# Attention weights turned by 32 x 32 squares and a copy through DRAM, with later weight conversions spaced out

## The chip, the cores and the metric

One core of a Trainium2 chip runs the whole program. The metric is the device time of one execution in microseconds. Engines are named as in the profile: PE (TensorE matmul), PEld (its weight load), DVE (VectorE), ACT (ScalarE), POOL (GpSimd), SP (SyncE, which here only issues DMAs).

## The reference, cut to what matters

Sliding-window attention over 4 batches, 8 heads, 576 positions of 64 elements, window 64, and after it two gated two-layer networks over the 2304 tokens:

```python
scores = (q @ k.T) / sqrt(64), masked to 0 <= i - j < 64
attn = softmax(scores)
x = (attn @ v) as [2304, 512]
x = (silu(x @ w_gate) * (x @ w_val)) @ w_out              # 512 -> 1536 -> 512
out = (sigmoid(x @ w_gate2) * (x @ w_val2)) @ w_out2      # 512 -> 1536 -> 512
```

The network weights arrive as 64-bit floats (read as pairs of 32-bit words); the kernel makes float32 of them itself.

## The kernel before, in words

**Tiling.** The 2304 tokens are 18 attention blocks of 128 tokens (i = 0 to 17). They feed five token tiles of 4, 3, 4, 4 and 3 blocks (512 or 384 columns). The first network runs over the five tiles in turn, then the second network does. One pass over a tile is a stage; stages 0 to 4 are the first network's. A stage walks over 12 chunks of 128 hidden units, and each chunk is three slots on PE: the gate product `g` (12 matmuls, L429), the value product `v` (12 matmuls, L429), and the out product `a` of the chunk before (12 matmuls, L441). So a stage has 36 slots, numbered through, and slot 36 opens stage 1. Each product is made of three terms of high and low parts, so weights and activations are split into two tiles by ACT (the high part, L411 and L707) and DVE (the low part, L415 and L621).

**Order of the work.** The order on every engine is written out by hand. Three tables, `before`, `during` and `after`, say which steps are emitted ahead of a slot's product, behind it, and behind the slot's activation. Every engine and every DMA queue works strictly in its own order. `g` and `v` have one PSUM bank each, so a product waits until ACT (L696) or DVE (L705) has read the one three slots earlier. The low part of a chunk's hidden tile (L621) is emitted two slots after its `v` slot, and the out product needs it at its third matmul, four slots after that `v` slot.

**Attention inside the stages.** Blocks 0 to 3 come ahead of stage 0. While tile t is in the network, the blocks of tile t+1 are planned by `plan_attention(i, base, t, col)`: loads at base-2, q and k turned at base+1, scores on PE ahead of slot base+2 (L244), mask and row minimum on DVE after base+2 and base+3 (L263), exponentials on ACT after base+3 (L279), normalization on DVE after base+4 and base+5 (L292 to L294), the weights transposed on PE ahead of slots base+7 and base+8 (L302, four 128 x 128 transposes each) and copied out by ACT (L308), and the product with v ahead of slot base+9 or base+10 (L318), whose result is split into the next tile's x (L328, L331). For i below `TURN` (8) q and k are transposed by PE too (L202) and copied by ACT. For later blocks, q and k are copied from DRAM to DRAM into an order by 32 x 32 squares (`to_squares`, L133, two DMAs per call), loaded in that order (L145) and turned by two DVE transposes (L231).

**Weights.** The first network's weights are converted during stage 0. The second network's 36 tiles are converted in stages 2 and 3, one every two slots: a 512 KB load (L359) into one of four `raw` buffers, two ACT instructions (`round_a`, L377 and L380), four DVE instructions (`round_b`, L388 to L391), and a 256 KB store (L397). A reload (`tw`, L402) of an out-weight tile runs in every chunk. All DMAs of the stages are issued by SP; POOL issues none.

## Time and profile before

| what | value |
|---|---|
| runs | 1000.22, 1001.97, 1002.98 us; median 1001.97 |
| profiled execution | 1002.0 us, span 1000.2 us, mean granted clock 0.986 |
| stage 0 on PE | about 40.7 to 165.7 us, with the first network's conversions |
| stage 1 (384 columns, blocks 7 to 10) | 165.67 to 254.97 us |
| stage 2 (512 columns, blocks 11 to 14) | 254.97 to about 367 us |
| stage 3 (512 columns, blocks 15 to 17) | about 367 to 474 us |

The profiled execution's own time is 1.8 us above its span, which is what lies around the first and the last instruction. A time of the timeline is counted from the start of the span. A window's busy time can't exceed its length; a share of DMA near 1 means that all 16 DMA engines had packets all the time.

### The profile page before, as it was taken

To read this page: it belongs to the slowest core of one execution; us is meant where nothing else is said; L and a number is where in the kernel's file an instruction comes from. 1 tells how busy PE (TensorE), PEld (TensorE's weight loads), DVE (VectorE), ACT (ScalarE), POOL (GpSimd) and SP (SyncE) were. 2 spreads that over 40 slices of the span, in tenths; PEclk is the share of its full clock that TensorE was granted. 3 is DMA by queue.
4 is the path that set the end of the run, shared out by engine and by line. 5 is a ranking of instruction groups with operands and counts; after the bars stand their busy time and mean duration, and the time that the engine had idled before them with its cause. 6 is when DMAs were issued, how large, how long until landed. Compare 5 with 4: busy or idle time off the path is not lost.

```text
span 1000.2 us, 14684 instructions
## 1 busy us (share of the span) xinstructions
PE 980.4 (98%) x5621; PEld 844.7 (84%) x5621; DVE 515.6 (52%) x1181; ACT 457.0 (46%) x981; POOL 4.1 (0%) x20
## 2 busy tenths in 40 slices
PE   8899999999999999999999999999999999999998
PEld 6678778999888888888999888899988888888997
DVE  6999994545677768666555322233322222223322
ACT  6887785555666555655444222222222222222222
POOL 1000000000000000000000000000000000000000
PEclk7999999999999999999999999999999999999999
DMA  9658797962366667464554400020020002000100
GB/s 224 193 179 221 216 240 171 223 148 80 116 212 186 209 206 232 164 205 137 200 148 126 169 0 1 1 85 1 1 74 1 1 1 74 0 1 1 42 1 32
DMA packets 164982, 113.03 MB, mean 113 GB/s; under 512 B 102704, under 2 KB 139568, under 8 KB 164912
## 3 DMA queue, kind: packets, MB, share of 16 engines
q1 hardware_dynamic: 161264, 111.18, 38.4%
q10 hardware_dynamic: 3648, 0.92, 0.4%
q8 instruction: 44, 0.72, 0.3%
q14 instruction: 26, 0.21, 0.1%
HBM read 90.05 MB, written 27.53 MB: 118 GB/s over the span
## 4 chain that ended last, share of the span: by engine, by line
PE 86%; DVE 9%; issue 2%; DMA 1%; ACT 1%; SPq 0%; DVEq 0%
PE a L441 28%; PE g L429 27%; PE v L429 27%; DVE raw L388 2%; PE att L318 1%; DVE t L390 1%; PE att L244 1%; PE att L302 1%; DVE t L391 1%; DVE t L389 1%; DVE z L263 1%; DVE h L621 1%; DVE s L705 1%; DMA raw<-in_moe_w_val_dram 1%; DVE wv L415 0%
## 5 line engine op out<-in xcount | busy, mean ns | idle before, releaser
L429 PE MATMUL g<-x,wg 128*128 128x512 f32 (+1 forms) x1440 | 317.8, 369 | 0.7 <-ACT x L328 0.7
L429 PE MATMUL v<-x,wv 128*128 128x512 f32 (+1 forms) x1440 | 317.6, 369 | 0.0
L429 PEld LDWEIGHTS g<-x,wg 128*128 128x128 f32 x1440 | 263.3, 188 | 37.5 <-ACT x L328 0.8
L429 PEld LDWEIGHTS v<-x,wv 128*128 128x128 f32 x1440 | 261.1, 188 | 33.1
L705 DVE TENSOR_TENSOR s<-s,v 128x512 f32<-128x512 f32 (+1 forms) x120 | 75.9, 632 | 318.3 <-PE v L429 305.9
L696 ACT ACTIVATE s<-g 128x512 f32<-128x512 f32 (+1 forms) x120 | 66.5, 554 | 312.9 <-PE g L429 312.7
L441 PE MATMUL a<-h,wo 128*128 128x512 f32 (+1 forms) x720 | 166.4, 380 | 6.4 <-DVE h L621 6.4
L441 PE MATMUL a<-wo,h 128*128 128x512 f32 x648 | 157.4, 390 | 0.0
L441 PEld LDWEIGHTS a<-h,wo 128*128 128x128 f32 x720 | 132.3, 192 | 27.0 <-DVE h L621 7.6
L707 ACT ACTIVATE h<-s 128x512 fp32r<-128x512 f32 (+1 forms) x120 | 70.6, 588 | 180.6 <-DVE s L705 180.6
L441 PEld LDWEIGHTS a<-wo,h 128*128 128x128 f32 x648 | 121.3, 188 | 24.2
L621 DVE TENSOR_TENSOR h<-s,h 128x512 fp32r<-128x512 f32 (+1 forms) x120 | 76.1, 634 | 3.2
L388 DVE TENSOR_SCALAR raw<-raw 128x512 uint16<-128x512 uint16 x72 | 54.0, 750 | 9.0 <-ACT raw L377 9.0
L279 ACT ACTIVATE z<-z,nm 128x128 f32<-128x128 f32 x144 | 55.8, 389 | 2.9 <-DVE nm L263 2.7
L101 DVE TENSOR_TENSOR x<-rx,x 128x512 fp32r<-128x512 f32 (+1 forms) x20 | 12.8, 639 | 84.3 <-ACT x L100 84.3
L391 DVE CUSTOM_DVE_ANT_0 t<-raw,t 128x1024 uint16<-128x1024 uint16 x72 | 49.8, 692 | 2.5
L380 ACT ACTIVATE t<-raw 128x512 f32<-128x512 f32 x72 | 47.9, 666 | 0.0
L377 ACT ACTIVATE raw<-raw 128x512 int32<-128x512 uint32 x72 | 47.9, 666 | 0.0
L415 DVE TENSOR_TENSOR wo<-stay,wo 128x512 fp32r<-128x512 f32 x60 | 41.1, 684 | 0.0
L411 ACT ACTIVATE wo<-stay 128x512 fp32r<-128x512 f32 x60 | 37.4, 624 | 0.0
L415 DVE TENSOR_TENSOR wo<-tw,wo 128x512 fp32r<-128x512 f32 x48 | 32.9, 685 | 5.7 <-ACT wo L411 5.7
L389 DVE TENSOR_SCALAR t<-t 128x512 f32<-128x512 f32 x72 | 33.3, 463 | 0.0
(84 smaller groups left out, 562.7 us busy)
## 6 DMA issues: line engine op xcount, KB each, us to landing
raw<-in_moe_w_gate_dram SPq DMA_DIRECT2D x24, 512.0 KB, 4.2
raw<-in_moe_w_val_dram SPq DMA_DIRECT2D x24, 512.0 KB, 4.4
raw<-in_moe_w_out_dram SPq DMA_DIRECT2D x24, 512.0 KB, 3.8
tw<-k0o SPq DMA_DIRECT2D x48, 256.0 KB, 4.2
v<-in_v_dram SPq DMA_DIRECT2D x29, 256.0 KB, 4.5
out_dram<-o SPq DMA_DIRECT2D x18, 256.0 KB, 2.3
k<-ks SPq DMA_DIRECT2D x10, 384.0 KB, 5.3
k0o<-t SPq DMA_DIRECT2D x12, 256.0 KB, 2.2
```

Of the source, the lines that this page charges most:

```text
L279: nc.scalar.activation(out=z[:, hp, :], in_=z[:, hp, :], func=ACTF.Exp, scale=-1.0, bias=nm[:, hp:hp + 1], accum_out=su[:, hp:hp + 1],)
L377: nc.scalar.activation(out=lower, in_=lower.bitcast(UINT32), func=ACTF.Copy, scale=2.0 ** -29)
L380: nc.scalar.activation(out=t.bitcast(FP32), in_=upper.bitcast(FP32), func=ACTF.Abs)
L388: nc.vector.tensor_scalar(second, fourth, 0x8000, 0x4000, ALU.bitwise_and, ALU.bitwise_or)
L391: nc.vector.tensor_tensor(out=t, in0=t, in1=lower, op=ALU.add)
L415: nc.vector.tensor_tensor(out=w[:, 1], in0=mids.pop(key), in1=w[:, 0].bitcast(FP32), op=ALU.subtract)
L429: nc.tensor.matmul(out=ps[:, 0:n], lhsT=w[:, a, c, :], rhs=xt[:, b, c, 0:n], start=(j == 0), stop=(j == len(mm) - 1),)
L441: nc.tensor.matmul(out=acc[e][:, 0:n] if m == 0 else acc[e], lhsT=w[:, a, cols] if m == 0 else h[:, a, cols], rhs=h[:, b, 0:n] if m == 0 e ...
L621: nc.vector.tensor_tensor(out=h[:, 1, 0:n], in0=s, in1=h[:, 0, 0:n].bitcast(FP32), op=ALU.subtract)
L696: nc.scalar.activation(out=s, in_=gps[:, 0:n], func=(ACTF.Silu, ACTF.Sigmoid)[m])
L705: nc.vector.tensor_tensor(out=s, in0=s, in1=vps[:, 0:n], op=ALU.mult)
L707: nc.scalar.activation(out=h[:, 0, 0:n], in_=s, func=ACTF.Copy)
```

## The change

Seven edits. `TURN` is 7 instead of 8, so block 7 also takes its q and k by squares. For blocks from 7 on, the softmax weights are no longer transposed by PE and copied by ACT: DVE turns them square by square into one tile (`turn_p`, twice per block, after slot base+5), POOL's queue writes that tile to DRAM (`put_p`, one DMA of 512 KB, in slot base+6) and reads it back with the squares exchanged between partition groups (`get_p`, four DMAs of 128 KB, in slot base+7); the product with v reads the result with a strided access pattern. Both new tiles come from the four `raw` buffers. That product is now ahead of slot base+12 for these blocks, and the base of blocks 8 and later is 3 smaller, so its slot stays where it was for most of them; everything ahead of it in the block moves three slots forward. The preceding half of v goes into another buffer (`pt0`) and is loaded in slot base+7. The second network's conversions start in stage 1 (slot 38) and come one every three slots, each with its own load two slots ahead.

```diff
     NTL = len(BLOCKS)
     last = min(range(NTL), key=lambda t: (BLOCKS[t], -t))
     ORDER2 = [t for t in range(NTL) if t != last] + [last]
-    TURN = BLOCKS[0] + BLOCKS[1] + 1
+    TURN = BLOCKS[0] + BLOCKS[1]
     TILES = []
     t0 = 0
     for n in BLOCKS:
@@ -150,7 +150,7 @@

     def load_before(i, pool=None):

-        pool, eng = (pool, nc.scalar) if pool else ((qt_p, "qt"), nc.sync)
+        pool, eng = (pool, nc.scalar) if pool else ((p_p, "pt0") if i >= TURN else (qt_p, "qt"), nc.sync)
         if i:
             nat[i, "v0"] = load_tokens(v, "v0", 128 * i - W, pool, 0, eng)
         else:
@@ -308,6 +308,33 @@
         nc.scalar.activation(out=t, in_=ps, func=ACTF.Copy)
         st[i, "pt", par] = t

+
+
+    def turn_p(i, par):
+        z, _ = st.pop((i, "z", par))
+        if par == 0:
+            st[i, "zt"] = raw_p.tile([128, 4, 2, HP, 32], FP32, tag="raw", name="zt")
+        nc.vector.transpose(st[i, "zt"][:, :, par].rearrange("p j a r -> p a j r"), z)
+
+    def put_p(i):
+        d = dram.tile([4, 32, 4, 2 * HP * 32], FP32, name=f"pd{i}")
+        nc.gpsimd.dma_start(
+            out=d.rearrange("i c j e -> (i c) (j e)"),
+            in_=st.pop((i, "zt")).rearrange("p j b a r -> p (j b a r)"),
+        )
+        st[i, "pd"] = d
+
+    def get_p(i):
+        d = st.pop((i, "pd"))
+        t = raw_p.tile([128, 4, 2, HP, 32], FP32, tag="raw", name="pt")
+        for j in range(4):
+            nc.gpsimd.dma_start(
+                out=t[32 * j:32 * j + 32].rearrange("c i b a r -> c i (b a r)"),
+                in_=d[:, :, j].rearrange("i c e -> c i e"),
+            )
+        for par in range(2):
+            st[i, "pt", par] = t[:, :, par].rearrange("p i a r -> p a i r")
+
     def pv(i, pick=None):
         ps = bank(pick)
         pt = [st.pop((i, "pt", par)) for par in range(2)]
@@ -318,7 +345,8 @@
                     nc.tensor.matmul(
                         out=ps[64 * par:64 * par + 64, hp, half * W:(half + 1) * W],
                         lhsT=vv[half][:, 2 * hp + par, :],
-                        rhs=pt[par][:, hp, half * W:(half + 1) * W],
+                        rhs=pt[par][:, hp, 2 * half:2 * half + 2] if i >= TURN
+                        else pt[par][:, hp, half * W:(half + 1) * W],
                         start=True,
                         stop=True,
                     )
@@ -487,11 +515,12 @@
             fn(*a)

     def plan_attention(i, base, t, col):
-        pv_at = 10 if t == 1 or (t > 2 and col == 0) else 9
+        pv_at = 12 if i >= TURN else 10 if t == 1 or (t > 2 and col == 0) else 9
+        base -= 3 * (i > TURN)
         if base >= 2:
             at(during, base - 2, load_qk, i)
         at(during, base + 1, load_v, i)
-        at(during, base + 5, load_before, i)
+        at(during, base + (7 if i >= TURN else 5), load_before, i)
         for nm in "qk":
             if i < TURN:
                 at(before, base + 1, transpose_in, i, nm)
@@ -506,8 +535,14 @@
         at(after, base + 4, normalize, i, 0)
         at(after, base + 5, normalize, i, 1, first=True)
         for par in range(2):
-            at(before, base + 7 + par, transpose_p, i, par)
-            at(before, base + 7 + par, evacuate_p, i, par)
+            if i < TURN:
+                at(before, base + 7 + par, transpose_p, i, par)
+                at(before, base + 7 + par, evacuate_p, i, par)
+            else:
+                at(after, base + 5, turn_p, i, par, first=True)
+        if i >= TURN:
+            at(during, base + 6, put_p, i)
+            at(during, base + 7, get_p, i)
         at(before, base + pv_at, pv, i)
         at(before, base + pv_at, lambda: x_hi(i, x_of(t), col))
         at(before, base + pv_at, lambda: x_lo(i, x_of(t), col))
@@ -536,11 +571,11 @@
         convs.append((3 * fc + 5, (0, "o", fc)))
     convs = [(n - 7, key) for n, key in sorted(convs)]
     later = [(1, nm, fc) for fc in range(FC) for nm in "gv"] + [(1, "o", fc) for fc in range(FC)]
-    convs += [(2 * SPT + 2 * j, key) for j, key in enumerate(later)]
+    convs += [(SPT + 2 + 3 * j, key) for j, key in enumerate(later)]
     next_raw = [0]

     def raw_ahead(upto):
-        while next_raw[0] < min(upto, len(convs)):
+        while next_raw[0] < min(upto, 3 * FC):
             load_raw(convs[next_raw[0]][1])
             next_raw[0] += 1

@@ -555,7 +590,10 @@
     for j, (s, key) in enumerate(convs[SPLIT_EARLY:], SPLIT_EARLY):
         at(during, s + 1, round_a, key)
         at(during, s + 2, round_b, key, key[0] == 1 or key[1] == "o")
-        at(during, s + 2, raw_ahead, j + 1 + 4)
+        if key[0] == 0:
+            at(during, s + 2, raw_ahead, j + 1 + 4)
+        else:
+            at(during, s - 2, load_raw, key)
         if key[0] == 0:
             plan_split(s + 2, key)
```

## Rows read from the trace of the kernel before

**Rows 1.** Page, part 1: busy time of each engine, share of the span, instructions.
```profile
PE 980.4 (98%) x5621; PEld 844.7 (84%) x5621; DVE 515.6 (52%) x1181; ACT 457.0 (46%) x981; POOL 4.1 (0%) x20
```

**Rows 2.** Windows: us, then each engine's busy us, granted clock, DMA share, GB/s.
```profile
125.00:150.00 25.00, 22.53 (x128) 17.79 (x127) 24.38 (x61) 20.24 (x45) 0.00 (x0) 0.98 0.96 240
165.67:254.97 89.30, 89.30 (x722) 85.56 (x721) 44.28 (x137) 48.41 (x122) 0.00 (x0) 1.00 0.58 139
187.80:209.90 22.10, 22.10 (x182) 21.29 (x181) 10.77 (x35) 11.83 (x30) 0.00 (x0) 1.00 0.70 150
254.97:367.00 112.03, 111.95 (x722) 91.04 (x722) 82.34 (x205) 70.75 (x158) 0.00 (x0) 1.00 0.63 193
```

**Rows 3.** Timeline of PE, stage 1: start us, us, line, operation, tiles, count [idle].
```profile
188.54 2.24 PE L429 MATMUL g<-x,wg 128*128 128x384 f32 x12
...
194.78 2.24 PE L429 MATMUL g<-x,wg 128*128 128x384 f32 x12
196.87 0.60 PE L302 MATMUL att<-ident,z 128*128 128x128 f32 x4
197.22 2.33 PE L429 MATMUL v<-x,wv 128*128 128x384 f32 x12
199.39 0.60 PE L302 MATMUL att<-ident,z 128*128 128x128 f32 x4
199.75 2.33 PE L441 MATMUL a<-h,wo 128*128 128x384 f32 x12
202.01 1.15 PE L318 MATMUL att<-pt,v 128*64 128x64 f32 x32
...
224.15 1.15 PE L318 MATMUL att<-pt,v 128*64 128x64 f32 x32
```

**Rows 4.** Timeline of PE, stage 2.
```profile
318.89 2.89 PE L429 MATMUL g<-x,wg 128*128 128x512 f32 x12
...
321.97 3.00 PE L429 MATMUL v<-x,wv 128*128 128x512 f32 x12
324.81 0.60 PE L302 MATMUL att<-ident,z 128*128 128x128 f32 x4
```

**Rows 5.** Timeline of PE, end of stage 0: the inputs of block 7.
```profile
156.92 0.66 PE L202 MATMUL att<-ident,q 128*128 128x128 f32 x4
158.41 0.65 PE L202 MATMUL att<-ident,k 128*128 128x128 f32 x4 [0.84 <-DVE x L331]
158.82 2.99 PE L429 MATMUL v<-x,wv 128*128 128x512 f32 x12
```

**Rows 6.** Timeline of DVE, stage 1, then a conversion in stage 2.
```profile
198.06 0.55 DVE L621 TENSOR_TENSOR h<-s,h 128x384 fp32r<-128x384 f32 x1
...
204.92 0.71 DVE L231 STREAM_TRANSPOSE qt<-q 128x512 f32<-128x512 f32 x1
205.54 0.94 DVE L231 STREAM_TRANSPOSE kt<-k 128x768 f32<-128x768 f32 x1
...
297.63 0.75 DVE L388 TENSOR_SCALAR raw<-raw 128x512 uint16<-128x512 uint16 x1
...
299.73 0.68 DVE L415 TENSOR_TENSOR wo<-tw,wo 128x512 fp32r<-128x512 f32 x1
```

**Rows 7.** PE after a wait in stage 0 (timeline), and that stretch's clock (windows).
```profile
107.62 4.14 PE L441 MATMUL a<-h,wo 128*128 128x512 f32 x10 [2.12 <-DVE h L621]
...
107.60:111.60 4.00, 3.98 (x10) 3.12 (x11) 3.93 (x8) 2.21 (x5) 0.00 (x0) 0.57 0.77 218
```

**Rows 8.** DMAs: landing of L359 and of L397; L133's issue, ns; medians 110 to 150 us.
```profile
DMA to landing us min/median/max: 3.4/4.2/7.2
...
DMA to landing us min/median/max: 2.0/2.2/5.6
...
L133 SPq DMA_DIRECT2D ks<-in_k_dram x48: 550/617/1545, 82.3 to 216.7; - x48
...
raw<-in_moe_w_val_dram SPq DMA_DIRECT2D x4, 512.0 KB, 5.3
```

## The prediction

> **What bounds the kernel now.** I read the page first, then windows by stage, then the timelines of PE, DVE, ACT and SP around one attention block, and last the DMA view. PE is busy 98% of the span [rows 1], so the end is set by the sum of PE's work plus its gaps. The windows say where the gaps are: late in stage 0 DVE is busy 24.4 of 25 us and PE 22.5; in stages 1 and 2 PE is full (89.30 of 89.30 and 111.95 of 112.03), while DVE is busy 50% and 74% and DMA 58% and 63% [rows 2]. So from 165.67 us on each microsecond of PE work that goes, or each microsecond that PE has to wait, moves the end by as much, if the cover of DVE and DMA holds.
>
> **What goes on PE.** In stage 1 a block's transposes take 0.35 and 0.36 us of start-to-start time (196.87 to 197.22, 199.39 to 199.75), and the products behind them are longer than the 2.09 us of the one ahead: 2.17 for `v`, 2.26 for `a` [rows 3]. Half of the last excess I leave to the entry into the product with v, which stays. That is 0.71 + 0.08 + 0.08 = 0.87 us per block. In stage 2 `g` and the transposes take 3.08 together, so `g` 2.73, and the `v` behind them 2.84 [rows 4]; with the second half alike 0.70 + 0.11 + 0.11 = 0.92. Blocks 7 to 10 lie in stage 1 and 11 to 17 in stages 2 and 3: 4 x 0.87 + 7 x 0.92 = 9.9 us. Block 7's q and k leave PE too: 156.92 to 158.82 is 1.90 us, 0.84 of it a wait [rows 5]. In its place DVE turns both, 0.62 + 0.94 us back to back [rows 6], behind the same x_lo that ended at 158.4; it ends near 160.0, and without the transposes PE reaches the scores at 159.65. So 0.3 us of wait comes back: 1.6 gained. Together 11.5 us.
>
> **What comes on DVE and ACT.** A conversion takes DVE 2.10 us from start to start (297.63 to 299.73), the two square turns of the weights 2 x 0.62 = 1.24, read from the q turn of the same 128 x 512 form [rows 6]; the new turns write in runs of 32 elements, for which no row has a price, and I take the same (twice that is 1.24 us more per block). Stage 1 gets 12 conversions and 4 pairs of turns: 44.3 + 25.2 + 5.0 = 74.5 us in about 85.7, that is 87%. This is between stage 2's 74%, where PE shows no loss, and stage 0's 98%, where it does [rows 2]. Stage 2 falls from 18 conversions to 12 and gets 5.0 us of turns: 82.3 - 12.6 + 5.0 = 75 us, covered better than now. ACT loses the two copies per block and gains 12 conversions in stage 1; it is 48.4 of 89.3 now and stays below 70%.
>
> One point of stage 1 is late all the same. The turns are queued on DVE ahead of the chunk's low part (L621). In block 8 that low part runs 198.06 to 198.61 behind the second normalization, and the out product at 199.75 needs it 0.35 later, at 200.1: 1.5 us to spare [rows 3, 6]. The turns take 1.24 of it, and PE arrives 0.8 sooner without its transposes: 0.5 us late, in blocks 8, 9 and 10, so 1.5 us. Block 7 has a 512-column out product there and is not late. In stages 2 and 3 each slot is 0.64 us longer [rows 3, 4], and the point stays covered.
>
> **The copy through DRAM.** This is the term that decides. From the end of the turns to the product with v there are 5 whole slots and the work of other blocks. Counted from the start of slot base+3, in stage 1: the turns end at 10.8 us (198.06 + 1.24, where that slot began at 188.54) [rows 3, 6]. The new block period is 22.14 (202.01 to 224.15) less 0.87, 21.3, and the product with v starts 1.1 before its end, at 20.2 [rows 3], or at 20.7 with the 0.5 us above. That leaves 9.8 us for the copy. Block 7 has no such 0.5, but 0.6 more in its 512-column out product: 10.0. In stages 2 and 3 nine slots are 5.8 us longer, the chain before the turns only 0.6 (its first product) to 2.7 (a conversion of 2.1 in it too): 12.5 to 14.6 us are left.
>
> Its cost has no row: POOL issues no DMA before. From SP's rows: a 256 KB store lands 2.2 us after issue, 512 KB loads 4.2 [rows 8]; for the other 256 KB of the store I add 1.0, a 512 KB read is 4.2, and three more issues in series at 0.62 each are 1.9: 9.3 us. The lower end takes the fastest landings (2.0 + 1.0 + 3.4 + 1.7 = 8.1). The upper end takes the slowest landings and issues (5.6 + 1.0 + 7.2 + 3 x 1.55 = 18.4). From 110 to 150 us, where DMA is nearly full, loads land in up to 5.3, 1.1 more than the median [rows 8]. Stage 1 gets as full: I add 0.85 to the store and to the read and take 11.0, nearest to the medians. So PE waits 11.0 - 9.8 = 1.2 us in three blocks of stage 1 and 1.0 in block 7: 4.6 us; none in stages 2 and 3.
>
> The Trainium skill prices this by its own rule ("DMA: Bandwidth & Descriptors", section "Anatomy of one DMA — SWDGE (gpsimd) path"): about 2.0 us fixed per DMA plus its bytes at 436 GB/s, and little for more descriptors. As an estimate from that page, the store is 3.2 us and the four reads, overlapped, 3 to 5, so the copy would fit and the sum would be 4.6 us lower. No run here shows it yet.
>
> DMA in stage 1: between 187.8 and 209.9 us it is busy 70%, 15.5 us [rows 2]. Per block come three 512 KB loads, three 256 KB stores and the copy's 1 MB; at stage 2's 193 GB/s per 0.63 share, 306 GB/s when full, that is 3.3 MB or 10.9 us: 26 us of work in 21.3, over slots 46 to 61, where the squares of the last batch are written. About 8 us would pile up. Loads have 3.5 slots (7.7 us) and need 4.2; behind them the activation has two slots. I count this as hidden apart from the 1.7 us above, with the whole 8 as a rival. The larger squares of batch 1 (slots 12 to 27) add about 1 MB to stage 0's nearly full DMAs; DVE is the bound there and finds its loads in time, so I take 0, and at most 2 us.
>
> Edits at no cost: the product with v reads two runs of 32 columns instead of 64 in a row (no row has it; each run is contiguous; at double its 1.1 us the price would be 12 us over 11 blocks); the `raw` buffers now carry five tiles per nine slots, each free at least one slot before its turn comes, SP and POOL waiting in order; conversions end in slot 145 and the first reload of them comes in slot 143 with the earliest of them.
>
> **Sum.** 1002.0 - 9.9 - 1.6 + 1.5 + 4.6 = 996.6 us. It is made on the profiled execution (1002.0), which equals the median of the runs, 1001.97; so the forecast is 996.6 us.
>
> **Rivals.**
> *The copy lands in time everywhere* (9.8 us or less): the medians' 9.3 speaks for it, the crowded stage 1 against. 996.6 - 4.6 = 992; without the late low parts 990.5.
>
> *The copy is held behind DVE's conversion burst, and PE's clock falls*: slower. Place: stage 1, slot base+6. Right behind the turns DVE does the low part and a conversion, 2.1 us without a pause. If POOL's queue can't start its store before that burst ends, the copy is 13.1 us and PE waits 3.3 per block. After a wait of 2.12 us in stage 0, ten matmuls took 4.14 us at a granted clock of 0.57, that is partly at the 1.2 GHz level [rows 7]; ten of them at the full level take 10/12 of 2.73, 2.3 us. So each such wait costs 1.8 more. A wait of 0.84 was followed by normal matmuls [rows 5]. Four blocks: 4 x (3.3 + 1.8) = 20; 992 + 20 = 1012. It decides from a copy of about 11.9 us, where the wait reaches 2.1: 4 x 3.9 = 16, 1008. For it: DVE's runs without a gap; against: the store may be handed out within the gaps.
> A rule of the Trainium skill says just that ("SBUF — State Buffer", section "Who interferes with whom"): a DMA issued from GpSimd's queue is starved while VectorE runs a copy or tensor-with-scalar instruction in a two-port mode, and should go by another queue. The conversion is made of four instructions like these; no row shows the starving, since POOL's queue moved nothing before.
>
> *DMA becomes the bound of stage 1's middle*: 8 us more than the case in time, 1000. For it the 26 us of work in 21; against, that stage 0 ran at 0.96 [rows 2] with no wait of ACT for a load.
>
> *DVE becomes the bound of stage 1*: if stage 1 behaves as stage 0, one wait of 2.1 us and its clock loss per block: 992 + 4 x 3.9 = 1007.
>
> **How the numbers follow.** No change means within 0.3%, 999.0 to 1005.0, about what a measurement of this kernel can tell. Forecast (copy late by up to 2 us in stage 1; own range 993 to 1000) 0.38; in time (989 to 993) 0.25; held behind the burst (1006 to 1015) 0.19; DMA the bound (997 to 1003) 0.13; DVE the bound (1003 to 1008) 0.05. Faster: 0.35 + 0.25 + 0.04 = 0.64; within: 0.03 + 0.09 + 0.02 + 0.02 = 0.16; slower: 0.20. The range 990 to 1006 leaves out about 0.04 below and 0.16 above.
>
> **What would show it.** Right: no L302 in blocks from 7 on, a block period near 22 us in stage 1 and 0.9 us shorter than before in stage 2; PE waits at L318 for a DMA near 1 us, in stage 1 alone. Wrong: waits of over 2 us at L318 with a granted clock below 1 behind them, or any such wait in stages 2 and 3; no wait at all at L318 (then 992); waits of ACT at L377 or L411 for DMAs (the DMA rival); PE waits at L441 for L621 of over 1 us in stage 1 (the DVE rival). The prediction is wrong where the time is above 1006, or where a gain comes from stage 0.

## The result, and the profile after

The changed kernel takes 1016.08 us (median of 4 runs, 1014.42 to 1020.03) beside 1001.5 for the kernel before in the same measurement: a ratio of 1.0144, 95% interval 1.0111 to 1.0178. It is slower, and it lies outside the predicted range. The profiled execution is the slowest of the four, with a span of 1018.2 us; before had 1000.2.

The page first. PE's work went down by 2.4 us against [rows 1], while the span went up by 18: PE waits, and part of its work runs slower.

```profile
PE 978.0 (96%) x5525; PEld 841.6 (83%) x5525; DVE 529.9 (52%) x1205; ACT 445.2 (44%) x956; POOL 45.2 (4%) x75
```

The windows by stage say where (columns as in [rows 2]: length, busy time of PE, PEld, DVE, ACT, POOL, granted clock, DMA share, GB/s). The stages are cut at the first product `g` of each.

```profile
166.94:273.49 106.55, 91.94 (x690) 87.41 (x689) 70.57 (x190) 59.29 (x146) 13.37 (x20) 0.94 0.87 236
195.00:213.00 18.00, 17.73 (x152) 16.97 (x154) 11.10 (x27) 7.22 (x12) 2.74 (x5) 0.85 1.01 260
224.00:240.00 16.00, 12.89 (x115) 11.63 (x113) 10.23 (x25) 4.70 (x9) 3.36 (x5) 0.89 1.04 289
273.49:492.10 218.61, 214.09 (x1281) 174.51 (x1281) 144.01 (x344) 113.22 (x250) 27.79 (x35) 0.99 0.63 194
196.20:200.90 4.70, 4.70 (x33) 4.58 (x31) 2.91 (x6) 1.74 (x3) 1.11 (x3) 0.57 1.08 264
```

Stage 1 was 89.30 us with PE full [rows 2]; it is 106.55 now, 17.25 longer, with PE idle for 14.6. Stages 2 and 3 together are 218.61, against 219.2 before (254.97 to 474.2): 0.6 shorter, where the prediction had 6.4. From stage 4 on nothing changed (526.1 us, 526.0 before). Stage 0 is 1.3 longer in this profile, which is not the change: the twelve profiles taken here with block 7's inputs on squares have 121.8 to 126.4 us there, median 123.3, and the five with them on PE 125.0 or 125.1.

The timeline of PE shows the idle time of stage 1: start, duration, what it computes, and in brackets the wait ahead of it with what ended it.

```profile
181.05 1.10 PE L244 MATMUL att<-kt,qt 64*64 64x128 f32 x32 [2.81 <-DVE kt L231]
...
195.27 1.98 PE L345 MATMUL att<-pt,v 128*64 128x64 f32 x32 [4.59 <-DMA pt<-pd]
197.18 3.77 PE L457 MATMUL g<-x,wg 128*128 128x384 f32 x12
...
225.03 2.03 PE L469 MATMUL a<-h,wo 128*128 128x384 f32 x10 [0.41 <-DVE h L659]
...
233.93 1.59 PE L244 MATMUL att<-kt,qt 64*64 64x128 f32 x32 [2.70 <-DVE kt L231]
235.44 3.44 PE L469 MATMUL a<-h,wo 128*128 128x384 f32 x12
...
264.53 1.51 PE L345 MATMUL att<-pt,v 128*64 128x64 f32 x32 [3.70 <-DMA pt<-pd]
265.97 3.51 PE L457 MATMUL g<-x,wg 128*128 128x384 f32 x12
```

L345 is the product with v (L318 before), L457 and L469 are `g`/`v` and `a` (L429 and L441), L659 the low part of h (L621). Two waits are for the copy (4.59 and 3.70 us), two for the turned q and k of a block (2.81 and 2.70), and 0.8 us in all for the low part of h. Behind three of the four long ones PE is slow: `g` takes 3.77 us where [rows 3] have 2.24, at a granted clock of 0.57 (the last window row above), partly at the 1.2 GHz level. With the clock at 1.00 stage 1 has 86.3 us of PE work (v4 and v6 below); here it is 91.94. So 17.25 = 14.6 of waits + 5.6 of slow clock - 3.0 of work that went.

Why block 8's q and k are late is a matter of order on DVE (first wait above). Block 8 starts 3 slots ahead, block 7 does not, so 6 slots lie between them where the others have 9, and block 8's inputs are queued behind block 7's normalization and turns:

```profile
177.08 0.69 DVE L294 TENSOR_TENSOR z<-z,su 128x512 f32<-128x512 f32 x1
177.69 1.30 DVE L317 STREAM_TRANSPOSE zt<-z 128x512 f32<-128x512 f32 x2
178.91 0.51 DVE L659 TENSOR_TENSOR h<-s,h 128x384 fp32r<-128x384 f32 x1
179.34 0.70 DVE L231 STREAM_TRANSPOSE qt<-q 128x512 f32<-128x512 f32 x1
179.97 0.93 DVE L231 STREAM_TRANSPOSE kt<-k 128x768 f32<-128x768 f32 x1
```

Block 10's q and k are late for another reason: DVE itself stood until their loads had landed.

```profile
231.68 0.71 DVE L231 STREAM_TRANSPOSE qt<-q 128x512 f32<-128x512 f32 x1 [2.99 <-DMA q<-qs]
232.80 0.98 DVE L231 STREAM_TRANSPOSE kt<-k 128x768 f32<-128x768 f32 x1 [0.41 <-DMA k<-ks]
```

These two loads landed 5.9 and 6.3 us after their issue; in stage 1 of the kernel before, such loads landed in medians of 4.0 and 4.8. SyncE was also issuing one DMA right behind another from 218.5 to 236.8 us, so a part of the lateness can be that queue's backlog. No run separates the two.

The copy of block 7 in POOL's timeline:

```profile
179.29 0.71 POOL L321 DMA_DIRECT2D pd<-zt  x1 [172.74 <-DVE zt L317]
185.89 2.64 POOL L331 DMA_DIRECT2D pt<-pd  x4 [5.90 <-DMA v<-in_v_dram]
```

The DMA issues of stage 1 (count, KB each, median us from issue to landing):

```profile
raw<-in_moe_w_val_dram SPq DMA_DIRECT2D x6, 512.0 KB, 6.1
raw<-in_moe_w_gate_dram SPq DMA_DIRECT2D x6, 512.0 KB, 4.3
pd<-zt POOLq DMA_DIRECT2D x4, 512.0 KB, 4.7
...
pt<-pd POOLq DMA_DIRECT2D x16, 128.0 KB, 5.2
k<-ks SPq DMA_DIRECT2D x5, 384.0 KB, 6.3
```

The turns end at 179.0 and the store is issued 0.3 us later. The loads are issued at 185.89, 0.6 us after the store has landed (the view puts the wait down to another DMA of that moment), and take 2.64 us to issue. Where PE waited for the copy, the turns were 16.3 us (block 7) and 13.7 us (block 10) behind it. Raw loads of `w_val` land in 6.1 us, where [rows 8] had 5.3 in the crowded stretch of stage 0; those of `w_gate` land in 4.3.

### The profile page after: what moved, and what is told of

Its sections match the earlier page's. It is cut to its first block, busy times and chain, and to the rows that moved or that the text cites. A ratio compares the mean times of both kernels' runs of the same rounds, so it can differ in the third digit from the quotient of the medians.

```text
span 1018.2 us, 14634 instructions
## 1 busy us (share of the span) xinstructions
PE 978.0 (96%) x5525; PEld 841.6 (83%) x5525; DVE 529.9 (52%) x1205; ACT 445.2 (44%) x956; POOL 45.2 (4%) x75
## 4 chain that ended last, share of the span: by engine, by line
PE 77%; DVE 10%; DMA 5%; ACT 3%; issue 3%; SPq 1%; POOL 1%; DVEq 0%; ACTq 0%
PE g L457 25%; PE a L469 24%; PE v L457 23%; DMA pt<-pd 2%; DVE raw L416 2%; PE att L345 1%; ACT z L279 1%; DVE t L418 1%; DMA raw<-in_moe_w_out_dram 1%; PE att L244 1%; DVE t L419 1%; DVE t L417 1%; DVE z L263 1%; DVE h L659 1%; DVE s L743 1%
## 5 line engine op out<-in xcount | busy, mean ns | idle before, releaser
L457 PE MATMUL g<-x,wg 128*128 128x512 f32 (+1 forms) x1440 | 324.9, 375 | 0.7 <-ACT x L356 0.7
L457 PE MATMUL v<-x,wv 128*128 128x512 f32 (+1 forms) x1440 | 316.2, 368 | 0.0
L457 PEld LDWEIGHTS g<-x,wg 128*128 128x128 f32 x1440 | 268.7, 192 | 38.8 <-ACT x L356 0.8
L457 PEld LDWEIGHTS v<-x,wv 128*128 128x128 f32 x1440 | 262.0, 188 | 33.5
L469 PE MATMUL a<-h,wo 128*128 128x512 f32 (+1 forms) x720 | 165.6, 378 | 7.1 <-DVE h L659 7.1
L745 ACT ACTIVATE h<-s 128x512 fp32r<-128x512 f32 (+1 forms) x120 | 70.6, 588 | 199.0 <-DVE s L743 199.0
L469 PE MATMUL a<-wo,h 128*128 128x512 f32 x648 | 157.4, 390 | 0.0
L469 PEld LDWEIGHTS a<-h,wo 128*128 128x128 f32 x720 | 132.7, 192 | 28.8 <-DVE h L659 9.5
L469 PEld LDWEIGHTS a<-wo,h 128*128 128x128 f32 x648 | 121.3, 188 | 24.2
L659 DVE TENSOR_TENSOR h<-s,h 128x512 fp32r<-128x512 f32 (+1 forms) x120 | 75.9, 632 | 3.9
L359 DVE TENSOR_TENSOR x<-att,x 128x512 fp32r<-128x512 f32 x14 | 9.7, 691 | 45.4 <-ACT x L356 45.4
```

The lines of the kernel that those rows point to most:

```text
L457: nc.tensor.matmul(out=ps[:, 0:n], lhsT=w[:, a, c, :], rhs=xt[:, b, c, 0:n], start=(j == 0), stop=(j == len(mm) - 1),)
L469: nc.tensor.matmul(out=acc[e][:, 0:n] if m == 0 else acc[e], lhsT=w[:, a, cols] if m == 0 else h[:, a, cols], rhs=h[:, b, 0:n] if m == 0 e ...
L659: nc.vector.tensor_tensor(out=h[:, 1, 0:n], in0=s, in1=h[:, 0, 0:n].bitcast(FP32), op=ALU.subtract)
L745: nc.scalar.activation(out=h[:, 0, 0:n], in_=s, func=ACTF.Copy)
```

## The experiments

Theory: in stage 1 the DMA engines have more work than PE, through the conversions and the copy together, and the wait falls on whatever transfer is late. Rivals: the copy's queue on GpSimd, the order of SyncE's queue, the pressed block starts. One table for all, from window rows like those above. DMA work is the share times the length, that is the time that the packets took, per DMA engine. A packet's whole time is counted where it starts, so a share can pass 1. The work is 3.7 to 4.2 us per MB in every row, and highest in the kernel before: the crowding has not swollen it.

| kernel | stage 1 us | PE busy | DMA work us | MB | stages 2+3 us | stage 4 us | ratio to before |
|---|---|---|---|---|---|---|---|
| before | 89.3 | 89.3 | 51.8 | 12.4 | 219.2 | 75.6 | 1 |
| changed | 106.6 | 91.9 | 92.7 | 25.1 | 218.6 | 75.6 | 1.0144 |
| e1 copy, no conversions in stage 1 | 94.7 | 86.7 | 70.1 | 18.1 | 236.7 | 75.6 | 1.0215 |
| e4 conversions, no copy | 92.0 | 90.6 | 77.3 | 20.5 | 219.1 | 75.6 | 1.0025 |
| e2 product with v later | 101.0 | 91.4 | 94.9 | 25.8 | 216.8 | 75.6 | 1.0061 |
| e3 q, k earlier | 108.3 | 93.2 | 99.7 | 26.0 | 217.7 | 75.6 | 1.0143 |
| e5 copy by ScalarE's queue | 110.5 | 91.3 | 90.6 | 24.5 | 213.5 | 75.6 | 1.0128 |
| e7 a quarter of raw bytes | 99.2 | 88.3 | 78.4 | 20.7 | 212.3 | 75.6 | 1.0028 |
| e8 stores by GpSimd's queue | 110.9 | 93.3 | 98.7 | 26.7 | 225.1 | 75.6 | 1.0249 |
| e9 starts mended | 103.2 | 92.0 | 95.0 | 25.3 | 217.9 | 75.6 | 1.0095 |
| v6 | 88.7 | 86.2 | 70.1 | 18.4 | 215.6 | 76.5 | 0.9942 |

**Each half alone.** e1 keeps the copy and puts the conversions back to where they were:

```diff
-    convs += [(SPT + 2 + 3 * j, key) for j, key in enumerate(later)]
+    convs += [(2 * SPT + 2 * j, key) for j, key in enumerate(later)]
```

> The changed kernel, with the later conversions back where they were (from slot 72, one every two slots). Theory A (the copy through DRAM is slow by itself: 13 to 16 us in every block against 9.8 us available in stage 1): PE still waits 3 to 5 us at the product with v in stage 1, with the clock falling behind it; the time stays at 1008 to 1016. Theory B (early conversions tie SP's queue to the pace of VectorE and fill the DMA engines in stage 1, and both late loads and slow copies follow from that): in stage 1 the waits for q and k go and the copy fits or is late by under 1 us; in stages 2 and 3, with 4.5 loads per block instead of 3, the copy may be later than now. 990 to 1000.

1023.93 us (1021.69 to 1028.4), ratio 1.0215, 1.0172 to 1.0257: above both ranges. Stage 1 loses 5.4 us against before in place of 17.25. But in stages 2 and 3 conversions in every second slot meet the copy, and the same thing happens there. Windows of e1: stage 1, then the stretch ahead of a wait of 4.14 us, the one behind it, and the stretch ahead of a wait of 4.38.

```profile
164.76:259.48 94.72, 86.69 (x689) 82.37 (x688) 48.41 (x146) 46.62 (x124) 11.14 (x20) 1.00 0.74 191
...
290.00:309.00 19.00, 14.51 (x94) 11.10 (x94) 13.77 (x31) 6.24 (x11) 3.50 (x5) 0.94 1.05 291
309.00:325.00 16.00, 16.00 (x89) 13.32 (x86) 9.99 (x27) 10.68 (x27) 0.70 (x1) 0.85 0.24 81
...
358.00:378.00 20.00, 15.19 (x99) 11.70 (x99) 14.43 (x34) 7.07 (x12) 3.49 (x5) 1.00 1.01 286
```

The share over the whole of stages 2 and 3 is 0.68, and yet it is full ahead of each wait and nearly empty behind one: the mean of a stage hides it. In e1's stage 1, without conversions beside them, the copies of blocks 7 to 10 took 11.5, 12.7, 10.7 and 10.7 us from the turns to the last landing, and PE waited for three of them: 2.28, 1.09 and 0.97 us.

e4 is the other half, the kernel before with the later conversions in stage 1:

```diff
-    convs += [(2 * SPT + 2 * j, key) for j, key in enumerate(later)]
+    convs += [(SPT + 2 + 3 * j, key) for j, key in enumerate(later)]
```

> The kernel before, with only the later conversions moved (from slot 38, one every three slots, each with its own load). Theory A: these alone cost little, 1000 to 1004, and stage 1 keeps its 89 us. Theory B: SP's queue is tied to VectorE already, q and k come late in stage 1 and PE waits there: stage 1 is 3 to 8 us longer, 1004 to 1010.

1004.71 us, ratio 1.0025 (1.0001 to 1.0049); stage 1 is 2.7 longer, a little under theory B's 3 to 8. So the halves cost 2.7 and 5.4 us in stage 1 and both together 17.25: 9 us belong to their meeting. In DMA work: the conversions add 25.5 us, the copy 18.3, either fits into 86 to 89 us of PE work, both do not.

**Moving the wait.** e2 gives the copy two slots more, e3 loads q and k earlier:

```diff
-        pv_at = 12 if i >= TURN else 10 if t == 1 or (t > 2 and col == 0) else 9
+        pv_at = 14 if i >= TURN else 10 if t == 1 or (t > 2 and col == 0) else 9
```
```diff
-            at(during, base - 2, load_qk, i)
+            at(during, base - (6 if i > TURN else 2), load_qk, i)
```

> The changed kernel, with the product with v two slots later (14 instead of 12 slots behind the base) for blocks 7 and later, which gives the copy 4.2 us more in stage 1 and 5.4 us more in stages 2 and 3. Theory A (the copy's length is the loss): the waits at the product with v (12.7 us in the profile of the changed kernel, and some 7 us of slow matmuls behind them) go except for 1 us at most; 996 to 1002, less what the late q and k still cost. Theory B (crowded DMA and SP's queue): the waits move to other places (q and k, the raw loads), at least half of the loss stays: 1006 to 1016.

> The changed kernel, with q and k of blocks 8 and later loaded four slots earlier. If the two waits of 2.7 to 2.8 us at the scores (with 1.6 us of slow matmuls) come from SP's queue standing behind the stores of the conversions, they go, and nothing else changes: 1008 to 1012 against 1016. If they come from full DMA engines, the loads land later too, or other transfers do, and the time stays within 3 us of 1016.

e2: 1009.69 us, ratio 1.0061 (1.004 to 1.0081). No wait for the copy is left, but stage 1 is still 101.0, with waits of 2.81, 2.28 and 2.22 us for turned q and k. Of the loss in time some two fifths stay, more than theory A and less than theory B said. e3: 1018.78, ratio 1.0143 (1.0085 to 1.0202), within 3 us of 1016 as the second side had it: block 10's wait for k is gone, and the product with v waits 5.01, 3.61 and 2.95 us in stage 1. In e3 what one transfer gains another loses; block 8's 2.81 stays in both.

**Which queue.** e5 issues store and loads from ScalarE, the loads a slot later:

```diff
-            at(during, base + 7, get_p, i)
+            at(during, base + 8, get_p, i)
...
-        nc.gpsimd.dma_start(
+        nc.scalar.dma_start(
```

> The changed kernel with the copy of the softmax weights (one store, four loads for each block) issued by ScalarE's queue in place of GpSimd's; the loads are issued one slot later, so that ScalarE doesn't stand behind the store. Theory (crowded DMA engines): the copy is as long as before, 12 us or more in stage 1 from the turn to the last landing (changed kernel: 13.4 to 16.3), pv still waits there for the copy, stage 1 stays at 103 us or more (106.6) and the time at 1011 to 1020 us. Rival (GpSimd's queue and its 2.2 to 2.9 us of issuing make the copy long): the copy takes 10 us or less from turn to landing, pv's waits for it go (10.6 us in the changed kernel), stage 1 comes to 98 us or less and the time to 1007 us or less.

1016.64 us, ratio 1.0128 (1.0089 to 1.0167), no gain. Waits of PE in the changed kernel (total us, times, longest):

```profile
PE att L345 <- DMA pt<-pd: 10.6, 3, 4.6
...
PE att L244 <- DVE kt L231: 5.5, 2, 2.8
```

And the first of e5's:

```profile
PE att L244 <- DVE kt L231: 12.3, 3, 8.7
```

Neither side is right in full. PE's waits for the copy fell in stage 1 from 8.3 to 3.1 us (0.96 in block 7 and 2.12 in block 10; the view puts these down to others, but they end 0.2 and 0.3 us behind the copy's last landing), and the time did not fall. q and k of a block now come 8.7 us late: SyncE's queue, which loads them, stood for 4.4 us behind the copy's store ahead of these loads. Such waits of SyncE's queue in stage 1 of e5 (in the changed kernel there is one, of 1.3 us):

```profile
SPq L145 <- DMA pd<-zt: 6.9, 1, 6.9
...
SPq L133 <- DMA pd<-zt: 4.4, 1, 4.4
```

So e5 shows that the move to ScalarE gains nothing as it stands, not that the queue costs nothing. The store lands in 3.0 us (median) from ScalarE's queue and 3.7 from GpSimd's, the loads in 5.2 and 5.4.

e6 leaves out DRAM and moves the weights from tile to tile, in 16 pieces of 32 KB:

```diff
         for j in range(4):
...
+            for i4 in range(4):
+                nc.scalar.dma_start(
+                    out=to[32 * j:32 * j + 32, i4], in_=z[32 * i4:32 * i4 + 32, j]
+                )
```

> The changed kernel with the softmax weights moved straight from the tile of turned squares to the tile that pv reads, 16 pieces of 32 KB issued by ScalarE's queue in slot 6, in place of the store to DRAM and the four loads: half of the copy's bytes, one transfer's landing in place of two. Everything else, the later conversions in stage 1 too, as in the changed kernel. Theory (the round trip's two landings on crowded DMA engines are the loss): the move lands 6 to 9 us after the turn, pv's waits for it (10.6 us and the clock behind them) go, the waits of scores for kt (5.5 us) stay, stage 1 is 93 to 98 us in place of 106.6 and the time 1003 to 1008 us. Rival (pieces of 32 rows by 1 KB are what is slow, or 16 issues hold ScalarE): the move takes 11 us or more, or ScalarE's issues take over 3 us for each block and show as waits of scores and products for ScalarE, and the time is 1012 us or more.

1123.11 us, ratio 1.1209: the rival. ScalarE's issuing is the price, and so the move's own length was not measured under comparable conditions. Timeline of ACT's queue in e6: eleven of a block's pieces take 8.09 us to issue, 0.74 each, and PE waits 101.8 us in all for `s` behind them.

```profile
177.61 8.09 ACTq L325 DMA_DIRECT2D pt<-zt  x11
```

e8 issues the stores of converted weights from GpSimd, so that no store on SyncE waits for DVE:

```diff
-            nc.sync.dma_start(out=d, in_=tf)
+            (nc.gpsimd if key[0] == 1 else nc.sync).dma_start(out=d, in_=tf)
```

> The changed kernel with the stores of the later converted weights issued by GpSimd's queue in place of SyncE's, so that SyncE's queue has no store left that waits for VectorE's conversion in stages 1 to 3; same bytes, same copy. Rival (the order of SyncE's queue holds the loads back): loads of q and k run ahead, the waits of scores for kt behind block 8 go, stage 1 is 100 us or less and the time 1010 us or less. Theory (DMA work of 92.7 us in a stage whose PE work is 86 to 87): the loss only changes its place, to the copy's loads behind a store in GpSimd's queue or to q and k; stage 1 at 104 us or more and the time 1013 to 1020 us.

1025.91 us, ratio 1.0249, worse than either side said. Waits for k behind block 8 are gone, as the rival wanted, and the copy's loads, queued behind the stores, cost more than before (waits of PE, e8):

```profile
PE att L345 <- DMA pt<-pd: 19.8, 9, 5.0
```

SyncE's raw loads stood 18.9 us behind the copy in stage 1 (1.3 in the changed kernel); both take the four `raw` buffers. So e8 mends one queue and burdens two.

**Fewer bytes, same order.** e7 loads a quarter of each later weight and lets GpSimd set the rest to zero, so it leaves out most of the second network's weights:

```diff
-        nc.sync.dma_start(out=dst, in_=rows(key))
+        src = rows(key)
+        if key[0] == 1:
+            n, size = (256, 1024) if key[1] == "o" else (1, CC)
+            nc.gpsimd.memset(dst[:, n:size], 0)
+            dst, src = dst[:, 0:n], src[:, 0:n]
+        nc.sync.dma_start(out=dst, in_=src)
```

> The changed kernel with a quarter of each later weight's bytes loaded (128 KB of 512 KB; GpSimd sets the other three quarters to zero, so that most of the second set of weights is left out); the conversions, their stores, the copy and the whole order as in the changed kernel. The share of the DMA engines in stage 1 times its length gives 51.8 us of DMA work before, 77.3 with the conversions alone, 70.1 with the copy alone and 92.7 in the changed kernel, whose PE work in stage 1 is 86 to 87 us. Theory (stage 1 became as long as its DMA work): about a dozen conversions fall there, some 8.1 MB with their stores, of which the loads left out are 4.6 MB or so, 14 us of the 25.5; the work is then some 78 us, below PE's: stage 1 is 95 to 99 us (what the copy alone gave, 94.7, and a little), the time 1005 to 1010 us. Rival (the order of SyncE's queue: stores that stand behind VectorE's conversions hold the loads of q, k and v back, whatever the bytes): stage 1 at 103 us or more, time 1013 us or more.

1004.81 us, ratio 1.0028 (1.0008 to 1.0048). DMA work came to 78.4 us, where 78 was expected, and stage 1 to 99.2, just over the upper end (99). Stages 2 and 3 show what the change is worth with no wait in them, 212.3 us with PE busy for all of it. Windows of e7, stage 1, and stages 2 and 3:

```profile
162.27:261.51 99.24, 88.35 (x689) 84.00 (x688) 76.40 (x190) 59.18 (x146) 21.75 (x31) 0.98 0.79 209
261.51:473.83 212.32, 212.32 (x1282) 173.31 (x1281) 154.98 (x344) 113.63 (x250) 38.92 (x59) 1.00 0.52 155
```

The rival does not fit: SyncE's queue stood longer behind the conversions than in the changed kernel, and stage 1 became shorter. Its waits for them in stage 1, changed kernel first, then e7:

```profile
SPq L425 <- DVE t L419: 21.2, 6, 9.9
...
SPq L430 <- DVE t L424: 28.4, 8, 6.0
```

One thing in e7 works against it. While GpSimd sets zeros, a conversion's first instruction on DVE takes up to 2.41 us (at most 0.77 in the changed kernel), and DVE is busy for 76.4 us in place of 70.6; so the bytes alone may be worth more. Of the 10.9 us of waits left, 2.8 are block 8's, and some 4 are for copies of 11.7 to 12.2 us, from the turns to the last landing, that had room for 10.0 to 11.7.

The window of stage 1 of e9, which comes next:

```profile
162.36:265.57 103.21, 91.97 (x689) 86.91 (x688) 71.31 (x192) 62.05 (x154) 11.97 (x20) 0.95 0.92 245
```

**The starts, with the conversions left in stage 1.** e9 mends the order of the blocks:

```diff
-        base -= 3 * (i > TURN)
+        base -= {TURN: 0, TURN + 1: 1, TURN + 2: 2}.get(i, 1 if nb == 3 else 3) if i >= TURN else 0
```
with the product with v at 14 slots (13 for a stage's last block and for blocks 12 slots apart) and q and k 5 slots ahead.

> The changed kernel with the starts alone altered, as in v4: blocks 8, 9 and 10 ahead by 1, 2 and 3 slots in place of 3 each, pv 14 slots behind a block's start (13 for the last block of a stage and where blocks are 12 slots apart), q and k of blocks from 8 on loaded 5 slots ahead. The later conversions stay one in 3 slots from stage 1 on. Theory (stage 1 has 92.7 us of DMA work, so that no order of the blocks can bring it below that): the 2.8 us wait of block 8 goes, others stay or move, stage 1 is 95 to 102 us, time 1004 to 1011 us. Rival (the pressed starts were the loss, DMA work only its shape): stage 1 at 91 us or less, time 1000 us or less.

1012.08 us, ratio 1.0095 (1.0068 to 1.0121). Block 8's wait falls from 2.81 to 0.64 us, and stage 1 is still 103.2: a little above the theory's end and 12 above the rival's. The three edits together are worth 3.3 us of stage 1 here, less than e2's later product alone (5.5), so the order's own worth is not known from e9. Of its 11.2 us of waits 5.0 are for the copy, and 2.83 for a low part of h that stood on DVE behind the turns. The bytes left out in e7 are worth 7.3, and order and conversions together (v4, v6) 17.7 and 17.8.

**Versions.** v1 has stage 1 as before and the copy from block 11 on, with the conversions one in 3 slots until stage 4; v2 the copy from block 7 on, mended starts and the same conversions:

```diff
+    convs += [(2 * SPT + 3 * j, key) for j, key in enumerate(later)]
```

> Stage 1 as in the kernel before (weights of blocks 7 to 10 transposed on TensorE, no later conversion there); the turned copy through GpSimd's queue from block 11 on alone, with pv 14 slots behind a block's start (13 where blocks are 12 slots apart); the later conversions one in 3 slots from stage 2 to stage 4, in place of one in 2 slots in stages 2 and 3. Theory (the copy is long only while it shares the DMA engines with the conversions and the loads of stage 1): stage 1 is 89 to 90 us as before (89.3), stages 2 and 3 are 212 to 215 us (219.2: 7 blocks by 0.92 us less), stage 4 grows by 1 us at most, time 993.5 to 998 us. Rival (the copy, DVE's turns and the new waits eat up what TensorE is spared, wherever they stand): stages 2 and 3 at 218 us or more, or stage 4 longer by 3 us or more, time 1000 us or more.

> The changed kernel with three things altered: the later conversions one in 3 slots from stage 2 to stage 4 (none in stage 1), pv 14 slots behind a block's start (13 where blocks are 12 slots apart), and the starts of blocks 8, 9 and 10 moved ahead by 1, 2 and 3 slots in place of 3 each, so that block 8 isn't pressed against block 7. Theory (what is lost in stage 1 is the DMA's crowding by conversions beside the copy, and the pressing of block 8 by a fixed 2.8 us): stage 1 is 85 to 89 us (106.6 in the changed kernel, 89.3 before), stages 2 and 3 are 212 to 215 us, time 989 to 996 us. Rival (stage 1 is full even without conversions, so that q, k and the copy hold one another up): stage 1 at 93 us or more with waits of 2 us and longer left on kt or on the copy, time 998 us or more.

v1: 1000.88 us, ratio 0.9989 (0.9968 to 1.001). Stage 1 is 89.4 as expected, stages 2 and 3 216.1 and stage 4 78.0, both over what I expected: PE waited 1.62 and 2.04 us for low parts of h that stood on DVE behind a conversion and a stage's output tiles, and 1.74 ahead of block 14's product with v, for which the trace names no cause. v2: 1011.1, ratio 1.0079 (1.0053 to 1.0104): the rival's figures, stage 1 95.6, because block 8's k, loaded 2 slots ahead, landed late (4.46 us); stages 2 and 3, at 220.5, are 5 over too, with three waits of 1.5 us for a low part of h among others.

v3 and v4 are these with the conversions one slot earlier, the output weights in every second slot of stage 4, and in v4 q and k 5 slots ahead:

> As v1 (stage 1 as before, the copy from block 11 on alone, pv 13 or 14 slots behind a block's start) with the later conversions moved by one slot against the h's low part (one in 3 slots through stages 2 and 3 for gate and value weights), and the output weights one in 2 slots from the 8th slot of stage 4. Theory (what v1 lost against 212.7 us of PE work in stages 2 and 3, and the 2.4 us of stage 4, were low parts of h that stood behind a conversion or behind stage 4's first output tiles): stages 2 and 3 213 to 215 us, stage 4 75.6 to 76.6, time 995 to 998 us, 0.4 to 0.7% below the kernel before. Rival (VectorE's turns hold the low part of h back by themselves): waits of 1.5 us for each block stay, stages 2 and 3 at 216 us or more, time 999 us or more.

> As v2 (the copy from block 7 on, no conversion in stage 1, blocks 8, 9 and 10 ahead by 1, 2 and 3 slots) with the conversions where v3 has them, q and k of blocks from 8 on loaded 5 slots ahead of a block's start in place of 2, and pv 13 slots behind the start for the last block of a stage. Theory (without conversions stage 1 has 70 us of DMA work beside 86 of PE; v2's 4.5 us wait was block 8's k, loaded too late): stage 1 86 to 89 us, stages 2 and 3 213 to 216 us, time 991 to 996 us. Rival (in stage 1 transfers come in bunches, so that any earlier load makes another one late): stage 1 at 92 us or more, time 998 us or more.

Both missed, in the main for one reason: v3 1003.94 us (1.0024, 1.0007 to 1.0041), v4 1005.33 (1.0047, 1.0025 to 1.0068). Stage 4 grew to 80.7 and 81.8, with waits of 0.3 to 1.1 us for a low part of h. Stage 1 did what was expected, 89.3 in v3 and 88.8 in v4; stages 2 and 3 were 0.2 and 2.3 over, at 215.2 and 218.3. So v5 and v6 start the conversions 10 slots ahead of stage 2 and leave nine, one in 3 slots, for stage 4:

```diff
+        (2 * SPT - 10 + 3 * j if j < 27 else (NTL - 1) * SPT + 6 + 3 * (j - 27), key)
```

> As v3, with the later conversions one in 3 slots from 10 slots ahead of stage 2 on (27 of them up to the end of stage 3), and the last 9 one in 3 slots from the 6th slot of stage 4. Theory (v3 lost 5 us in stage 4 to low parts of h behind a conversion in every second slot): stage 1 89.3 to 90.5 us, stages 2 and 3 214 to 216 us, stage 4 75.6 to 77 us, time 994.5 to 998.5 us beside 1000 to 1002 of the kernel before. Rival (conversions cost in stage 4 what they spare before it, at any spacing): stage 4 at 78 us or more, time 999 us or more.

> As v4 (the copy from block 7 on), with v5's places for the later conversions and q and k loaded 5 slots ahead for blocks 8 to 10 alone. Theory: stage 1 88.5 to 90.5 us (3 conversions at its end beside the copy), stages 2 and 3 214 to 216.5 us, stage 4 75.6 to 77 us, time 993.5 to 998 us. Rival (the three conversions beside block 10's copy bring the waits of stage 1 back): stage 1 at 92 us or more, time 999 us or more.

v5: 999.53 us, ratio 0.997 (0.995 to 0.999); its stages are as expected (89.6, 215.0, 75.6), the time is 1 us above. v6: 996.76 us (993.28 to 1000.76), ratio 0.9942 (0.9925 to 0.9959), in every range of its theory and faster than both kernels. Windows of v6, stage 1, and stages 2 and 3:

```profile
167.09:255.81 88.72, 86.23 (x689) 82.29 (x688) 51.20 (x151) 51.71 (x136) 11.11 (x20) 1.00 0.79 207
255.81:471.45 215.64, 212.93 (x1282) 173.52 (x1281) 146.60 (x351) 110.73 (x241) 25.13 (x35) 1.00 0.66 197
```

The copy is in all of v6's blocks from 7 on, by GpSimd's queue as in the changed kernel. The clock stays at 1.00, and 2.5 and 2.7 us of waits are left.

## Why the prediction was wrong

**The step that failed** is the DMA sum of stage 1. The prediction worked out 26 us of work in a period of 21.3 and 8 us of pile-up, and then went on: "I count this as hidden apart from the 1.7 us above". It was not hidden: stage 1 has 92.7 us of DMA work beside 86.3 of PE work. In the prediction's terms for stage 1: PE waits 8.3 us for the copy, where 4.6 were in the sum; 5.5 for the turned q and k, where there was nothing (2.8 of them, block 8's, are not DMA's, see below); 0.8 for the low part of h, where there were 1.5. That makes the 14.6 us of waits. The 5.6 us of slow clock behind them were in a rival only. The rival that took the 8 us whole had the place right and the price too low by more than half; and its sign, waits of ACT for raw weights, shows once, with 2.1 us. What came late were the copy and block 10's q and k. Stage 0, on which I leaned (share 0.96, no wait of ACT for a load), issues its raw loads four conversions ahead; the copy had no such lead.

**The copy at 11.0 us**: from the turns to the last landing it was 16.1, 11.8, 11.8 and 13.5 us in stage 1, against 11.5, 12.7, 10.7 and 10.7 in e1 and 9.8 to 14.1 in v4, both without conversions there. So 11.0 was near for e1, where PE waited 4.4 us in all for it (4.6 in the sum), and not for the changed kernel. The addition for a crowded stage, 1.7 us on top of 9.3, is the mis-sized term: it was 2.5 to 6.8. The room was predicted at 9.8 to 10.0; it was 10.0 in block 10, and 11.7 in block 7. Stages 2 and 3 were to have no wait for it: copies of 11.3 to 15.0 us met a room of 12.7 to 14.4, block 11 waited 2.29 and block 16 2.10 us.

**Block 8** was not seen. The prediction gave blocks 8 to 10 one period; the first of them has 6 slots and not 9. That is 2.81 us in the changed kernel and in each of e1, e2, e3, e5, e6, e7 and e8, which leave the starts alone, with conversions beside them or not.

**PE's transposes.** Predicted 0.92 us per block in stages 2 and 3, 6.4 in all: PE busy 219.15 before, 212.3 to 212.9 in e7, v1 and v6, so 6.2 to 6.8. Right. Stage 1: 3.5 predicted, 3.0 measured (89.3 to 86.3). The product with v reads its runs of 32 at no cost, as counted (median 0.222 us for one of its matmuls, before and after). The changed kernel got 5.1 of the 6.4 in stages 2 and 3 as PE work and lost 4.5 in waits.

**Block 7's inputs**, 1.6 predicted: 1.7 between the medians of stage 0 above, with 4.6 between the twelve profiles, so it agrees and is not shown. **The low part of h**, 0.5 us late in three blocks: 0.41 and 0.40 in two. Right.

**Held behind the burst.** Its forecast, 1012, is the nearest to the result, and that is luck: its mechanism is there, but small. In blocks 9 to 17 a conversion follows right behind the turns, and GpSimd takes 1.18 to 1.31 us to issue the store; in blocks 7 and 8, where none does, 0.71 and 0.56. The issue ends just behind the second of the conversion's four instructions, here in block 15 of the changed kernel, with block 15 of e1 below, where the conversion began earlier:

```profile
387.59 1.31 POOL L321 DMA_DIRECT2D pd<-zt  x1 [20.20 <-DVE zt L317]
...
387.79 0.74 DVE L416 TENSOR_SCALAR raw<-raw 128x512 uint16<-128x512 uint16 x1
388.32 0.45 DVE L417 TENSOR_SCALAR t<-t 128x512 f32<-128x512 f32 x1
388.81 0.43 DVE L418 TENSOR_SCALAR t<-t 128x512 int32<-128x512 int32 x1
...
392.41 0.71 POOL L321 DMA_DIRECT2D pd<-zt  x1 [22.93 <-DVE zt L317]
```

The first store lands in 3.7 us, the second in 3.1. So the hold is some 0.6 us, not the 2.1 that the rival took, and block 7, with the longest wait, has none. (Three of the four instructions work with a scalar, not all four as the prediction had it: the last adds two tensors.) What the rival had right is that a wait of over 2.1 us mostly brings a slow stretch behind it. The Trainium skill's rule on GpSimd's queue ("SBUF — State Buffer", "Who interferes with whom") would have the copy faster by another queue; e5 did that, the store landed 0.7 us sooner in the median, and the kernel took as long. The prediction's estimate from the Trainium skill ("DMA: Bandwidth & Descriptors", "Anatomy of one DMA — SWDGE (gpsimd) path"), 3.2 us for the store and 3 to 5 for the four loads, stands beside 3.7, and beside 7.7 from the first load's issue to the last landing (medians of all blocks).

**DVE as the bound**: 70.6 of 106.55 us busy in stage 1, where 74.5 were forecast, and its sign, a wait of over 1 us for the low part of h, is missing; no. What DVE did cost is the order behind block 8's wait.

What stays open: why the copies of stage 1 take 11.7 us and more even with DMA work below PE's (e7), and how much of the lateness of q and k is SyncE's backlog and how much the DMA engines'. e1's windows suggest bunches (1.05, then 0.24). That spreading the same transfers evenly would bring these stages down to PE's work was not tried. What is shown is that the halves alone cost 2.7 and 5.4 us of stage 1, that fewer bytes in the same order give back 7.3, and that with at most three conversions beside the copy, and with mended starts, the loss of stage 1 is gone (v4, v6).

## What to carry to other kernels

Before work is moved onto DMA, add up each stage's DMA work (share times length) with all parts of the change in it, and compare it with the bound engine's work in that same stage: two parts that cost 2.7 and 5.4 us alone cost 17.25 together. The sum warns, it does not give the time: e7, with 78.4 us of DMA work beside 88.3 of PE work, still took 99.2. Look at it in stretches of some 20 us as well, since a mean share of 0.68 held stretches that were full. And where a stage is full, giving one transfer more room hands much of the wait to the next one (all of it in e3, two fifths of the loss in e2); cutting bytes helped (e7), moving one of the parts to another stage helped most (v6).

## What the runs showed of the hardware

- DMA in the full stretches: the profile's share reaches 1.01 to 1.08 at 260 to 291 GB/s, in mostly small packets (in stage 1 of the changed kernel 42069 of 46558 are under 2 KB).
- The clock behind a wait is not decided by the wait's length alone: after 2.81 us the next products ran as usual in the changed kernel (1.10 at 181.05, granted clock 1.00) and slowly in e3 (1.99 for the same ones, 0.50); after 2.70 they ran slowly (1.59, 0.66). In stage 0, ten matmuls behind a wait of 2.11 us took 2.57 us in one place of the changed kernel's profile and 3.73 and 4.14 in two others (granted clock 1.00, 0.65 and 0.59).
- The first `g` of stage 0 took 3.0 to 3.1 us in fourteen profiles and 5.49 in three (the changed kernel, e5, v6). In these three PE had been idle for 2.0 us ahead of the last product before it, in the others for 0.9 to 1.3. These 2.4 us come and go between runs, which is a reason to compare stages and not only times.
- A DMA of 32 KB takes ScalarE 0.74 us to issue (e6); the four loads of the copy take GpSimd 2.2 to 2.9 us and ScalarE 1.8 to 2.1 in nine blocks of eleven.
- GpSimd and DVE hold each other up a little: the store's issue takes 0.56 to 0.71 us, and 1.18 to 1.31 with a conversion's first instructions right behind its start; beside GpSimd's zeros (e7) a conversion's first instruction takes up to 2.41 us, else at most 0.77.
